# Leaky sum kept in PSUM with its low half on VectorE, second conversions behind the next row maxima, and a respread transition and last step

## The chip, the cores and the metric

The kernel runs on one core of one Trainium2 chip. The metric is the device time of one launch in microseconds (us), given as the median of several runs. The engines are TensorE (PE in the profile, its weight loads PEld), VectorE (DVE), ScalarE (ACT), GpSimd (POOL) and SyncE (SP, which issues the DMAs).

## The reference

Sliding-window attention over 2 batches, 8 heads, 768 positions and head size 64, followed by two feed-forward layers over the 1536 tokens (512 wide, 2048 hidden). All is float32 to the reader of the output; the four weight matrices arrive as 64-bit floats.

```python
scores = scale * np.matmul(q, k.transpose(0, 1, 3, 2)) + bias          # bias: -slope[h] * distance
scores = np.where(is_global | is_local, scores, -1000000000.0)         # 8 global keys, the last 96 positions
a = np.exp(scores - np.max(scores, axis=-1, keepdims=True))
attn = np.matmul(a / (np.sum(a, axis=-1, keepdims=True) + 1e-09), v)
x = attn.transpose(0, 2, 1, 3).reshape(B * S, H * D)
h = x @ moe_w_in                                                       # layer 1
x = (np.maximum(h, 0.0) + alpha * np.minimum(h, 0.0)) @ moe_w_out
h = x @ moe2_w_in                                                      # layer 2
g = (a0 + a1*h + a2*h*h + a3*h*h*h) / (1 + |b0|*|h| + |b1|*h*h + 1e-6)
out = g @ moe2_w_out
```

## The kernel before

**Products.** Each float32 operand is held as a high and a low half of a reduced format, and a product is three passes: high times high, low times high, high times low. The high half is a copy into that format on ScalarE, the low half a subtraction.

**Steps.** A step is one block of 128 hidden columns for one group of 512 tokens. There are 96: 48 of layer 1, then 48 of layer 2, grouped into runs over the same tokens. `first(n)` is the step's product with w_in: 12 matmuls into one PSUM bank `h` (bank 3 for the first 16 steps, later banks 0 to 2 in rotation). Then comes the nonlinear part: in layer 1 `leaky(n)`, in layer 2 the `rational_*` functions, called a, u, b, c, p, d, h, e here (a, u, c, h on ScalarE, b, p, d on VectorE, e on GpSimd). Both end in a high half `ghi` and a low half `glo`. `second(n)` is the product with w_out, 12 matmuls into banks 4 to 7, which add up over a run. At a run's end `drain` takes the four banks out; in a run's last step `second` finishes bank after bank and so wants the low half with its third matmul. Where a run's sum is part of an earlier one (`adds`), VectorE adds the saved part (L826), ScalarE copies the high half, and the low half (L835) is put off into the queue `later`.

**Slots.** The order of every engine's instructions is written out by hand (`tc.manual_schedule`), and each engine works its own list in order. While attention runs, slot s of 16 (`joint_slot`) issues: `opening` (scores of the next rows, reciprocals L472 and row maxima L447 of VectorE, exponentials L454 of ScalarE, values), `first(s)`, a tick, `turning` (transposes of the probabilities, their copies out, the split of new keys and queries L408 and L411), `leaky(s)`, `second(s-1)`, a tick. Afterwards a plain slot s issues `first(s)`, the nonlinear part of step s-1 and the end of that of s-2, a tick, `second(s-2)`, a tick. `final_slot` does the last step in two column halves.

**Ticks and conversions.** There are two ticks to a slot, number 2s and 2s+1. A tick moves the conversion of weights on: a 64-bit block of 128 x 512 is scaled by ScalarE (L324) in the tick at which it starts, joined into float32 by three VectorE instructions (L313, L314, L315) in the next, copied to its high half by ScalarE (L301) in the third and subtracted for its low half by VectorE (L304) in the fourth. `plan_weights` lists the ticks at which the blocks start; for layer 2 these are `times`. A tick also takes one entry from `later`.

The instructions of `leaky` are L741 and L742 on VectorE, L743 on ScalarE, L744 on GpSimd; those of `rational_d` L777 to L779, of `rational_h` L782, of `rational_e` L786.

Of the kernel before, what the change touches and what calls it, by code (L numbers as in the profile page):

```python
# [60 lines left out]
class Kernel:  # L61
# [35 lines left out]
    def arm(self, attention, sfx):  # L97
        tc = self.tc
        self.sfx = sfx
        self.slots = list(self.early)  # L100
        self.pipe, self.join, self.unspilled, self.later, self.splits = (deque() for _ in range(5))
        self.loads = self.started = self.used = 0
        moe = self.moe()
        with tc.tile_pool(name="spill_" + sfx, bufs=1, space=DRAM) as spill:
            self.spilled = [self.alloc_slot(spill, i, "d") for i in range(KEPT)]
            self.saved = {mg: spill.tile([P, NC, DM], F32, name=f"saved{mg[0]}{mg[1]}_{sfx}") for mg in SAVED}
            with tc.tile_pool(name="at_" + sfx, bufs=1) as pool:
                attention(pool, moe)
            with tc.tile_pool(name="late_" + sfx, bufs=1, reuse_waits="tile") as late:
                self.slots += [self.alloc_slot(late, i) for i in range(NEARLY, NF)]  # L110
                moe(None)
# [109 lines left out]
    def plan_weights(self):  # L221
        self.steps = [(0, 0, fc, fc % NEARLY) for fc in range(CH)]
        self.steps += [(0, 1, fc, fc % NEARLY) for fc in (*range(NEARLY, CH), *range(NEARLY))]
        self.steps += [(0, 2, fc, fc) for fc in range(NF)]
        self.steps += [(0, g, fc, fc) for g in (0, 1) for fc in range(CH, NF)]
        self.steps += [(1, g, j, j) for g in (2, 0) for j in range(CH)]
        self.steps += [(1, 1, j, j) for j in range(NF)]
        self.steps += [(1, g, j, j) for g in (2, 0) for j in range(CH, NF)]
        runs = [s[:2] for s in self.steps]
        self.begins = {n for n in range(len(runs)) if n == 0 or runs[n - 1] != runs[n]}  # L230
        self.ends = {n - 1 for n in self.begins if n} | {len(runs) - 1}
        self.saves = {n for n in self.ends if runs[n] in runs[n + 1 :]}
        self.adds = {n for n in self.ends - self.saves if runs[n] in SAVED}
        jobs = {}
        for fc in range(CH):
            jobs[2 * fc - 5 if fc > 2 else 2 * fc - 10] = 0, fc, "in", fc % NEARLY
            jobs[2 * fc - 2 if fc else -5] = 0, fc, "out", fc % NEARLY
        half, layer = NGR * CH, NGR * NF
        spare = [(fc, kind) for fc in range(CH, NF) for kind in ("in", "out")]
        for t, (fc, kind) in enumerate(spare):  # L240
            jobs[11 + 2 * t if fc < KEPT else 15 + 2 * t] = 0, fc, kind, None if fc < KEPT else fc
        todo = []
        for n, free in ((0, LATE), (CH, layer - CH)):
            for k in range(CH):
                for kind, lag in (("in", 0), ("out", 5)):
                    todo.append((n + k, 2 * (free + k) + lag, kind))
        times = [t for t in range(48, 96) if (t % 2 == 0 or t in (55, 71) or t > 82) and t not in (64, 66, 80, 82, 85, 88, 91, 94, 95)]
        times += range(101, 160, 5)
        for t in times:
            ready = [x for x in todo if x[1] <= t]  # L250
            if ready:
                j, _, kind = job = min(ready)
                todo.remove(job)
                jobs[t] = 1, j, kind, j
        assert not todo
        self.starts = set(jobs)
        self.plan = [jobs[t] for t in sorted(jobs)]
# [25 lines left out]

    def tick(self, on_act, start, spread=False):
        nc = self.nc
        if self.later:
            self.later.popleft()()
        while self.splits:
            self.splits.popleft()()
# [431 lines left out]
    def moe(self):  # L721
# [16 lines left out]
        def leaky(n):  # L738
            fc, h = steps[n][2], hbank.pop(n)
            t, hi, lo = self.act[n % 2], self.ghi[n % 2], self.glo[n % 2]  # L740
            nc.vector.tensor_scalar(t, h, 0.0, self.al[:, fc : fc + 1], ALU.min, ALU.mult)  # L741
            nc.vector.scalar_tensor_tensor(t, h, 0.0, t, ALU.max, ALU.add)  # L742
            nc.scalar.copy(hi, t)  # L743
            nc.gpsimd.tensor_tensor(lo, t, hi.bitcast(F32), ALU.subtract)  # L744

        def rational_parts(n):
            p = flat[NST - 2 + n % 2]
# [62 lines left out]
        def drain(n, d):  # L810
            m, g = steps[n][:2]
            y, o, r0 = banks[4 + d], self.part[d], g * GT + d * P
            out = self.out[r0 : r0 + P, :]
            if n in self.saves:
                if n < LATE - 1:
                    o = self.first_saved[d]
                (nc.vector.tensor_copy if d == 3 and m else nc.scalar.copy)(o, y)  # L817
                nc.sync.dma_start(out=self.saved[m, g][:, d, :], in_=o)
                return
            if n == N - 1 and d == 3:  # L820
                for half in (slice(0, DM // 2), slice(DM // 2, DM)):
                    nc.vector.tensor_add(o[:, half], y[:, half], o[:, half])
                    nc.sync.dma_start(out=out[:, half], in_=o[:, half])
                return
            if n in self.adds:
                nc.vector.tensor_add(o, y, o)  # L826
            elif m:
                (nc.vector.tensor_copy if d == 3 else nc.scalar.copy)(o, y)
            if m:
                nc.sync.dma_start(out=out, in_=o)  # L830
                return
            xh, xl = self.xhi[g][:, d, :], self.xlo[g][:, d, :]
            if n in self.adds:
                nc.scalar.copy(xh, o)
                self.later.append(lambda: nc.vector.tensor_sub(xl, o, xh.bitcast(F32)))  # L835
            else:
                nc.scalar.copy(xh, y)
                nc.vector.tensor_sub(xl, y, xh.bitcast(F32))
# [6 lines left out]
        def joint_slot(s, halves):  # L845
# [4 lines left out]
            if s == LATE - 1:  # L850
                self.spill()
            opening(u)
            first(s)
            self.tick(True, 2 * s in self.starts)
            lows = turning(u)
            leaky(s)
            for low in lows:
                low()
            if s:
                second(s - 1)  # L860
            self.tick(True, 2 * s + 1 in self.starts)

        def plain_slot(s):
            early, late = s - 1, s - 2
            fetch(s + 1)
            if CH <= s - LATE + CH - 2 < KEPT:
                self.reload(s - LATE + CH - 2)
            if s < N:
                first(s)
            if s >= N:  # L870
                final_slot(s)
                return
# [10 lines left out]
                rational_b(early)  # L883
            if late >= LATE and steps[late][0]:
                rational_e(late)
            if ready and not steps[early][0]:
                leaky(early)
            self.tick(True, 2 * s in self.starts)
            if ready and steps[early][0]:
                rational_c(early)  # L890
                rational_p(early)
# [83 lines left out]
```

## Time and profile before

| what | value |
|---|---|
| median of 3 runs | 663.15 us (661.48 to 663.91) |
| the profiled execution | 662.42 us |
| its span, first to last instruction | 660.6 us |
| TensorE busy | 622.9 us, 94% of the span |
| VectorE busy | 541.1 us, 82% |
| ScalarE busy | 374.8 us, 57% |
| GpSimd busy | 191.6 us, 29% |

The span is read on the slowest core, here the only one. Busy shares are means over the span; the stages have different limits, so the stretches of single slots tell more than the totals. A matmul's duration overlaps the next one's, so TensorE is read by its start times and by the waits in front of its instructions.

### The profile page before, as it was taken

How to read it: one execution, taken by the hardware profiler on the slowest of the kernel's cores; microseconds unless marked ns; L12 is line 12 of the kernel's file. 1: busy time of each engine (PE TensorE's matmuls, PEld its weight loads, DVE VectorE, ACT ScalarE, POOL GpSimd, SP SyncE). 2: the span in 40 equal slices, each digit the busy share in tenths (PEclk: the TensorE clock that was granted, in tenths of full speed). 3: DMA queues.
4: the chain of work that ended last, by engine and by line, in shares of the span. 5: the costliest groups of instructions: out<-in, count | busy, mean ns of one | idle time of the engine just before them, and what ended most of it. 6: DMA issues, size and time to landing. Idle time of an engine off the chain costs nothing. (4 is left out here: it accounts for less than half of the span.)

```text
span 660.6 us, 9551 instructions
## 1 busy us (share of the span) xinstructions
PE 622.9 (94%) x3250; PEld 506.3 (77%) x3250; DVE 541.1 (82%) x972; ACT 374.8 (57%) x782; POOL 191.6 (29%) x268
## 2 busy tenths in 40 slices
PE   6777998999999999999999998999999999999994
PEld 6566766778878888888888877878878888888783
DVE  4687899987656987977889999999989877786984
ACT  2785565667643432333333376777777666766662
POOL 4454434333341321222222212222222222222221
PEclk7998999999999999999999999999999999999998
DMA  8879498978777952330522511131110000300302
GB/s 162 192 189 274 145 256 261 269 207 268 255 263 253 353 183 90 103 96 32 165 90 65 158 34 33 36 125 32 33 64 1 1 1 1 127 1 0 129 0 70
DMA packets 84859, 82.82 MB, mean 125 GB/s; under 512 B 45312, under 2 KB 61952, under 8 KB 84800
## 3 DMA queue, kind: packets, MB, share of 16 engines
q1 hardware_dynamic: 84800, 82.11, 41.6%
q8 instruction: 27, 0.44, 0.3%
q14 instruction: 32, 0.26, 0.1%
HBM read 60.21 MB, written 19.92 MB: 121 GB/s over the span
## 5 line engine op out<-in xcount | busy, mean ns | idle before, releaser
L744 POOL TENSOR_TENSOR glo<-act,ghi 128x512 fp32r<-128x512 f32 x48 | 65.6, 1366 | 213.5 <-ACT ghi L743 193.8
L786 POOL TENSOR_TENSOR glo<-act,ghi 128x512 fp32r<-128x512 f32 (+1 forms) x49 | 65.3, 1332 | 201.9 <-ACT ghi L782 180.3
L743 ACT CAST ghi<-act 128x512 fp32r<-128x512 f32 x48 | 29.8, 621 | 104.6 <-DVE act L742 96.7
L735 PE MATMUL bank<-xhi,winhi_f 128*128 128x512 f32 x256 | 68.4, 389 | 0.0
L735 PE MATMUL bank<-xhi,winlo_f 128*128 128x512 f32 x256 | 68.4, 389 | 0.0
L735 PE MATMUL bank<-xlo,winhi_f 128*128 128x512 f32 x256 | 68.4, 389 | 0.0
L454 ACT ACTIVATE prob<-prob,stat 128x232 f32<-128x232 f32 (+1 forms) x96 | 44.7, 468 | 40.2 <-DVE stat L447 40.0
L735 PEld LDWEIGHTS bank<-xhi,winhi_f 128*128 128x128 f32 x256 | 48.1, 188 | 10.0
L735 PEld LDWEIGHTS bank<-xlo,winhi_f 128*128 128x128 f32 x256 | 48.1, 188 | 10.0
L735 PEld LDWEIGHTS bank<-xhi,winlo_f 128*128 128x128 f32 x256 | 48.1, 188 | 10.0
L314 DVE SCALAR_TENSOR_TENSOR dx<-de,dx 128x512 int32<-128x512 int32 x64 | 52.7, 824 | 2.2
L315 DVE SCALAR_TENSOR_TENSOR dx<-stage,dx 128x512 int32<-128x512 int32 x64 | 52.1, 815 | 2.2
L762 DVE SCALAR_TENSOR_TENSOR stage<-stage,abs_b 128x512 f32<-128x512 f32 (+1 forms) x49 | 36.2, 739 | 16.3 <-ACT stage L754 16.3
L753 ACT ACTIVATE stage<-bank 128x512 f32<-128x512 f32 (+1 forms) x49 | 28.8, 587 | 35.7 <-PE bank L735 35.7
L466 POOL TENSOR_SCALAR prob<-prob,rec 128x232 f32<-128x232 f32 (+1 forms) x96 | 42.2, 458 | 16.9 <-DVE rec L472 10.2
L782 ACT CAST ghi<-act 128x512 fp32r<-128x512 f32 (+1 forms) x49 | 30.2, 616 | 27.7 <-DVE act L779 27.7
L324 ACT ACTIVATE de<-stage 128x512 f32<-128x512 f32 x64 | 42.6, 671 | 2.6 <-DMA stage<-in_moe_w_out_dram 2.6
L801 PE MATMUL bank<-wouthi_f,glo 128*128 128x512 f32 x144 | 41.3, 392 | 0.8 <-POOL glo L786 0.7
L801 PE MATMUL bank<-wouthi_f,ghi 128*128 128x512 f32 x144 | 41.3, 392 | 0.6 <-ACT ghi L782 0.6
L313 DVE TENSOR_SCALAR dx<-de 128x512 int32<-128x512 int32 x64 | 38.6, 603 | 3.5 <-ACT de L324 3.5
L801 PE MATMUL bank<-woutlo_f,ghi 128*128 128x512 f32 x144 | 41.0, 389 | 0.0
L777 DVE SCALAR_TENSOR_TENSOR stage<-stage,cq,bank 128x512 f32<-128x512 f32 (+1 forms) x49 | 36.0, 734 | 4.1 <-ACT bank L767 4.1
(208 smaller groups left out, 1466.7 us busy)
## 6 DMA issues: line engine op xcount, KB each, us to landing
stage<-in_moe_w_in_dram SPq DMA_DIRECT2D x32, 512.0 KB, 3.9
stage<-in_moe_w_out_dram SPq DMA_DIRECT2D x32, 512.0 KB, 4.1
part<-saved_f SPq DMA_DIRECT2D x16, 256.0 KB, 4.0
va<-in_v_dram SPq DMA_DIRECT2D x13, 256.0 KB, 5.1
saved_f<-part SPq DMA_DIRECT2D x12, 256.0 KB, 3.5
out_dram<-part SPq DMA_DIRECT2D x11, 256.0 KB, 2.0
rawk<-in_k_dram SPq DMA_DIRECT2D x10, 256.0 KB, 4.6
rawq<-in_q_dram SPq DMA_DIRECT2D x10, 256.0 KB, 4.7
```

The lines of the kernel that those rows point to most:

```text
L313: lambda: nc.vector.tensor_scalar(y, e, 3, None, ALU.logical_shift_left),
L314: lambda: nc.vector.scalar_tensor_tensor(y, e, -(2**31), y, ALU.bitwise_and, ALU.bitwise_or),
L315: lambda: nc.vector.scalar_tensor_tensor(y, low, 29, y, ALU.logical_shift_right, ALU.bitwise_or),
L324: nc.scalar.mul(self.de[n % 2], self.staged(n)[:, :, :, 1].bitcast(F32), 2.0**-112)
L454: nc.scalar.activation(p[:, j - e, :w], p[:, j - e, :w], AF.Exp, bias=st[:, j : j + 1], scale=-1.0, accum_out=st[:, 4 + j : 5 + j],)
L466: nc.gpsimd.tensor_scalar(p[:, j, :w], p[:, j, :w], r[:, e + j : e + j + 1], 1.0, ALU.mult, ALU.mult)
L735: nc.tensor.matmul(bk, w["in", a][:, c, :], x[:, c, :], start=e == 0, stop=e == len(seq) - 1)
L744: nc.gpsimd.tensor_tensor(lo, t, hi.bitcast(F32), ALU.subtract)
L762: nc.vector.scalar_tensor_tensor(w, w, self.ab[:, 0:1], ab, ALU.add, ALU.mult)
L777: nc.vector.scalar_tensor_tensor(w, w, self.cq[:, 0:1], r, ALU.add, ALU.mult)
L786: nc.gpsimd.tensor_tensor(lo, u, hi.bitcast(F32), ALU.subtract)
L801: nc.tensor.matmul(y[d], lhs, rhs, start=begin and e == 0, stop=last and e == 2)
```

## The change

- `leaky` writes its sum back into the PSUM bank of `h`. ScalarE copies the high half from there, and the low half is a VectorE subtraction that reads that bank; GpSimd has no part in it any more. The function hands that subtraction back, and the caller places it: in a joint slot behind the low halves of keys and queries, in a plain slot behind the first tick.
- The odd tick of a joint slot stands behind the next slot's `opening` and not at the slot's end.
- `later` gives one entry at every other tick.
- The last conversions of layer 2 start at ticks 107, 112, ... and not 101, 106, ...
- `first` of the last step is issued one slot earlier.
- The last half block of the output is sent by ScalarE's DMA queue.

```diff
-        times += range(101, 160, 5)
+        times += range(107, 160, 5)
...
-        if self.later:
+        self.ticks += 1
+        if self.later and self.ticks % 2:
             self.later.popleft()()
...
             nc.vector.tensor_scalar(t, h, 0.0, self.al[:, fc : fc + 1], ALU.min, ALU.mult)
-            nc.vector.scalar_tensor_tensor(t, h, 0.0, t, ALU.max, ALU.add)
-            nc.scalar.copy(hi, t)
-            nc.gpsimd.tensor_tensor(lo, t, hi.bitcast(F32), ALU.subtract)
+            nc.vector.scalar_tensor_tensor(h, h, 0.0, t, ALU.max, ALU.add)
+            nc.scalar.copy(hi, h)
+            return lambda: nc.vector.tensor_sub(lo, h, hi.bitcast(F32))
...
-                    nc.sync.dma_start(out=out[:, half], in_=o[:, half])
+                    (nc.scalar if half.start else nc.sync).dma_start(out=out[:, half], in_=o[:, half])
...
             opening(u)
+            if s:
+                self.tick(True, 2 * s - 1 in self.starts)
             first(s)
             self.tick(True, 2 * s in self.starts)
             lows = turning(u)
-            leaky(s)
-            for low in lows:
-                low()
+            low = leaky(s)
+            for more in lows:
+                more()
+            low()
             if s:
                 second(s - 1)
-            self.tick(True, 2 * s + 1 in self.starts)
+            if s == LATE - 1:
+                self.tick(True, 2 * s + 1 in self.starts)
...
-            if s < N:
+            if s < N - 1:
                 first(s)
+            if s == N - 2:
+                first(s + 1)
...
-            if ready and not steps[early][0]:
-                leaky(early)
+            low = leaky(early) if ready and not steps[early][0] else None
             self.tick(True, 2 * s in self.starts)
+            if low:
+                low()
```

In the changed file the same lines stand one number higher up to `leaky`'s, and its subtraction is L745.

VectorE at the seam of two joint slots, before: the leaky sum, the split of a query, then a conversion, then the next slot's reciprocals and row maxima.

```order
L742 SCALAR_TENSOR_TENSOR act_99<-bank_85,act_99 128x512
L411 SCALAR_TENSOR_TENSOR qlo_253<-bank_84,qhi_251 128x512
L304 TENSOR_TENSOR woutlo__122<-dx_96,wouthi__121 128x512
L313 TENSOR_SCALAR dx_98<-de_94 128x512
L314 SCALAR_TENSOR_TENSOR dx_98<-de_94,dx_98 128x512
L315 SCALAR_TENSOR_TENSOR dx_98<-stage_90,dx_98 128x512
L472 RECIPROCAL rec_263<-rec_263 128x4
L447 ISA prob_256,stat_261<-bank_82,bm_284 128x128
```

The same seam in the change, up to the last row maximum.

```order
L743 SCALAR_TENSOR_TENSOR bank_85<-bank_85,act_99 128x512
L412 SCALAR_TENSOR_TENSOR qlo_253<-bank_84,qhi_251 128x512
L745 TENSOR_TENSOR glo_103<-bank_85,ghi_101 128x512
L473 RECIPROCAL rec_263<-rec_263 128x4
L448 ISA prob_256,stat_261<-bank_82,bm_284 128x128
```

The conversion (now L305, L314 to L316) has moved behind the row maxima and the attention's low half, and `glo` is a VectorE instruction that reads bank_85, which is bank 3.

TensorE in the last three slots, before: the last step's first product (bank_84) stands behind step 92's second product, whose first matmul and last matmul are shown.

```order
L735 MATMUL bank_83<-xlo_108,winhi_f 128x512 x4
L801 MATMUL bank_86<-wouthi_f,ghi_101 128x512
...
L801 MATMUL bank_89<-wouthi_f,glo_103 128x512
L735 MATMUL bank_84<-xhi_105,winhi_f 128x512 x4
```

In the change:

```order
L736 MATMUL bank_83<-xlo_108,winhi_f 128x512 x4
L736 MATMUL bank_84<-xhi_105,winhi_f 128x512 x4
L736 MATMUL bank_84<-xhi_105,winlo_f 128x512 x4
L736 MATMUL bank_84<-xlo_108,winhi_f 128x512 x4
L802 MATMUL bank_86<-wouthi_f,ghi_101 128x512
```

The product into bank_84 has moved ahead of the twelve matmuls into banks 86 to 89.

VectorE at the layer change, before: the four sums of the drain, the first low half of `later`, then the three instructions of `rational_d`.

```order
L826 TENSOR_TENSOR part_78<-bank_89,part_78 128x512
L835 TENSOR_TENSOR xlo_109<-part_75,xhi_106 128x512
L777 SCALAR_TENSOR_TENSOR stage_92<-stage_92,cq,bank_85 128x512
L778 SCALAR_TENSOR_TENSOR stage_92<-stage_92,bank_85 128x512
L779 SCALAR_TENSOR_TENSOR act_99<-act_99,na,stage_92 128x512
L762 SCALAR_TENSOR_TENSOR stage_93<-stage_93,abs_b 128x512
L835 TENSOR_TENSOR xlo_109<-part_76,xhi_106 128x512
```

In the change:

```order
L827 TENSOR_TENSOR part_78<-bank_89,part_78 128x512
L778 SCALAR_TENSOR_TENSOR stage_92<-stage_92,cq,bank_85 128x512
L779 SCALAR_TENSOR_TENSOR stage_92<-stage_92,bank_85 128x512
L780 SCALAR_TENSOR_TENSOR act_99<-act_99,na,stage_92 128x512
L763 SCALAR_TENSOR_TENSOR stage_93<-stage_93,abs_b 128x512
L836 TENSOR_TENSOR xlo_109<-part_75,xhi_106 128x512
```

The first low half now follows `rational_d`, and the second has moved a slot on.

## Rows read from the trace of the kernel before

**Rows 1.** Windows by slot without attention: stretch, length, busy time per engine, PEclk, DMA.
```profile
300.57:306.01 5.44, 5.44 (x26) 4.50 (x24) 4.06 (x7) 1.89 (x4) 1.29 (x1) 1.00 0.00 0
...
387.61:394.86 7.25, 5.75 (x26) 4.43 (x24) 7.14 (x12) 6.77 (x13) 1.63 (x1) 1.00 0.00 0
...
400.36:407.99 7.63, 5.76 (x26) 4.43 (x25) 7.46 (x12) 5.83 (x10) 1.63 (x1) 1.00 0.24 69
429.75:436.20 6.45, 5.78 (x26) 4.43 (x24) 6.19 (x10) 3.97 (x8) 1.62 (x1) 1.00 0.26 92
441.64:447.45 5.81, 5.75 (x26) 4.43 (x24) 5.67 (x10) 3.93 (x8) 1.30 (x1) 1.00 0.29 90
480.13:485.96 5.83, 5.75 (x25) 4.37 (x24) 4.69 (x6) 4.59 (x9) 1.69 (x1) 1.00 0.46 155
485.96:492.54 6.58, 5.78 (x26) 4.43 (x25) 6.41 (x11) 5.32 (x10) 1.64 (x1) 1.00 0.00 0
601.34:606.77 5.43, 5.43 (x25) 4.50 (x24) 4.28 (x7) 3.52 (x7) 1.29 (x2) 1.00 0.00 0
```

**Rows 2.** Windows by slot, attention running, same columns.
```profile
99.57:109.67 10.10, 8.70 (x55) 6.38 (x53) 9.45 (x22) 6.06 (x18) 3.21 (x7) 1.00 0.93 266
...
158.35:167.26 8.91, 8.91 (x67) 7.30 (x65) 6.12 (x17) 5.71 (x16) 3.63 (x7) 1.00 0.98 284
```

**Rows 3.** Timeline of the slot at 99.57: start, us, engine, line, operands.
```profile
99.12 1.56 POOL L744 TENSOR_TENSOR glo<-act,ghi 128x512 fp32r<-128x512 f32 x1 [4.94 <-ACT ghi L743]
99.44 1.52 DVE L313 TENSOR_SCALAR dx<-de 128x512 int32<-128x512 int32 x1
...
102.33 0.17 DVE L472 RECIPROCAL rec<-rec 128x4 f32<-128x4 f32 x1
...
102.59 1.41 POOL L466 TENSOR_SCALAR prob<-prob,rec 128x128 f32<-128x128 f32 x4 [1.58 <-PE bank L735]
...
102.71 0.39 DVE L447 CUSTOM_DVE_ANT_0 prob<-bank,bm 128x232 f32<-128x232 f32 x1
...
105.17 0.42 DVE L313 TENSOR_SCALAR dx<-de 128x512 int32<-128x512 int32 x1
```

**Rows 4.** Groups by shape: busy us, mean ns, idle before.
```profile
L408 DVE TENSOR_TENSOR klo<-bank,khi 128x512 fp32r<-128x512 f32 x11 | 7.5, 685 | 3.1 <-ACT khi L407 3.0
```

**Rows 5.** Timeline of ScalarE in the slot of the last first product.
```profile
640.37 0.58 ACT L767 ACTIVATE bank<-bank 128x512 f32<-128x512 f32 x1
```

**Rows 6.** Timeline of VectorE in the slot at 79.43.
```profile
82.68 0.18 DVE L472 RECIPROCAL rec<-rec 128x4 f32<-128x4 f32 x1 [1.15 <-POOL rec L471]
```

**Rows 7.** Timeline of the slot at 158.35, with one conversion.
```profile
159.06 0.18 DVE L472 RECIPROCAL rec<-rec 128x4 f32<-128x4 f32 x1 [1.79 <-POOL rec L471]
...
161.31 0.68 DVE L304 TENSOR_TENSOR spare<-dx,spare 128x512 fp32r<-128x512 f32 x1
...
161.70 0.19 ACT L454 ACTIVATION_READ_ACCUMULATOR prob<-prob,stat 128x1 f32 x1
...
164.47 0.69 DVE L742 SCALAR_TENSOR_TENSOR act<-bank,act 128x512 f32<-128x512 f32 x1
```

**Rows 8.** Timeline of the layer change.
```profile
391.99 1.20 PE L801 MATMUL bank<-wouthi__113,ghi 128*128 128x512 f32 x4 [1.50 <-ACT ghi L782]
...
397.88 1.52 DVE L313 TENSOR_SCALAR dx<-de 128x512 int32<-128x512 int32 x1
...
400.78 0.68 DVE L772 TENSOR_TENSOR act<-act,bank 128x512 f32<-128x512 f32 x1
...
405.11 1.19 PE L801 MATMUL bank<-wouthi__121,ghi 128*128 128x512 f32 x4 [1.87 <-ACT ghi L782]
```

**Rows 9.** Timeline of the end.
```profile
642.83 0.38 ACT L753 ACTIVATE stage<-bank 128x256 f32<-128x256 f32 x1 [1.88 <-PE bank L735]
...
652.17 0.39 PE L801 MATMUL bank<-wouthi_f,glo 128*128 128x512 f32 x1
...
653.07 1.44 SPq L823 DMA_DIRECT2D out_dram<-part  x2
```

More of the change, by code (lines that the diff above doesn't have):

```diff
@@ L101, in arm @@
         self.pipe, self.join, self.unspilled, self.later, self.splits = (deque() for _ in range(5))
-        self.loads = self.started = self.used = 0
+        self.loads = self.started = self.used = self.ticks = 0
         moe = self.moe()
```

## Prediction

> **What bounds the kernel now.** I first read the windows by slot, because the stages have different limits. A plain slot (no attention) has 24 matmuls of 512 columns; in the typical ones at 300.57 and 601.34 TensorE is busy for all of 5.44 us, 0.2267 each, and nothing on another engine can shorten that [rows 1]. Six slots are longer: 7.25 and 7.63 us around the change of layer, 6.45 and 5.81, then 5.83 and 6.58 where the first two runs of layer 2 end. Their excess over 5.44 is 1.81 + 2.19 + 1.01 + 0.37 + 0.39 + 1.14 = 6.9 us. While attention runs the picture differs [rows 2]: the slot at 99.57 takes 10.10 us with TensorE busy for 8.70, and the slot at 158.35 takes 8.91 with TensorE busy throughout. The difference is the conversions: two per slot in the former, one in the latter.
>
> Second, the order of events in that 10.10 us slot [rows 3]. VectorE is busy 9.45 of 10.10 us [rows 2]; it is the limit there. One item is odd: the first conversion's L313 takes 1.52 us, the second's 0.42, for the same shape. The long one starts at 99.44, while GpSimd's subtraction L744 runs from 99.12 to 100.68, and it ends 0.28 after that. So GpSimd's low half costs VectorE 1.10 us per slot.
>
> Third, the timelines of the layer change and of the end, where each wait of TensorE has a releaser by name.
>
> **The low half on VectorE.** Removed: 48 GpSimd subtractions, 1.56 us each in rows 3, which lie beside other work but hold L313 for 1.10 us. Added: 48 VectorE subtractions with one input in PSUM and one in SBUF, output in SBUF. The nearest row is L408, the same kind: 0.685 us [rows 4]; behind others such an instruction starts about 0.6 after the one before it. The lower bound is 0.42 (the free L313, one input), the upper 1.52 (the held one) [rows 3]; I take 0.6. It also waits for ScalarE's copy of the high half, which starts only when L742 is done. L411 or L408 stands between and hides 0.6 of the copy's 0.6, so with the two hand-overs I allow 0.2. VectorE writing PSUM is in no row; between L408's 0.685 and L313's 1.52 I take no change, since ScalarE's pass from PSUM into PSUM, L767, takes 0.58 [rows 5] and shows no surcharge for that target.
>
> [...]
>
> Sum for a slot with two conversions: 10.10 - 1.10 + 0.6 + 0.2 = 9.8 us. In seven such slots (68 to 140 us) that is 7 x 0.3 = 2.1 us less.
>
> **The conversion behind the row maxima.** L472 and the four L447 now stand ahead of L313 to L315. GpSimd's normalisation L466, and with it TensorE's transposes, come some 2 us earlier in the slot; TensorE's wait in front of them goes. But the leaky sum now stays in bank 3 until the low half is read, and every joint slot's first product writes bank 3. In the old order first(s) started at 99.57, 2.8 us before L472 at 102.33 [rows 3]; in the new one it cannot start before the low half is done, just where L472 starts. So TensorE's wait moves from the transposes to first(s), and VectorE's 9.8 us stays the period. One slot pays more: at 82.68 L472 waits 1.15 us for GpSimd's copies of the global keys [rows 6]; the conversion that ran ahead of it is now behind, so VectorE stands idle about 1.3 us longer there. Joint stage: -2.1 + 1.3 = -0.8 us.
>
> For slots with one conversion I followed the same ring [rows 7]. ScalarE's exponentials end 2.83 us after L472 (161.89 - 159.06); the weight's high half, one ScalarE pass of about 0.6, now follows them and L304 waits for it, at +3.45; from L304's start to L742's end it is 3.85 (165.16 - 161.31); then copy 0.6 and the low half 0.6 to the next L472: 3.45 + 3.85 + 0.1 + 0.6 + 0.6 = 8.6 us. That is below 8.91, so these slots stay with TensorE. GpSimd no longer delays L471, which frees nothing that TensorE waits for here. In plain slots of layer 1 the added 0.6 is covered: TensorE takes 5.44 and VectorE 4.06 in the row at 300.57 [rows 1], and three banks rotate. Without that cover it would be 33 x 0.6 = 20 us.
>
> **Layer change.** `later` now gives one low half per slot, from the slot after the drains. Before, one L835 stands directly ahead of the three instructions that end in ScalarE's L782 (the order rows above show it), for which TensorE waits 1.50 us at 391.99 [rows 8]; taking it away brings 0.6. The conversion of tick 101, L313 at 397.88 to the next instruction at 400.78, is 2.9 us of VectorE ahead of the wait of 1.87 at 405.11; it moves three slots on, and the four L835 cost 0.6 in each of four slots where VectorE has about 1.1 to spare (5.44 less 4.28 at 601.34 [rows 1]). That slot loses its whole excess of 2.19. Together -2.8 us.
>
> **Runs' ends in layer 2.** All remaining conversions start six ticks later. Before, VectorE is exactly late at 405.11 and two conversions follow (ticks 106, 111) while a slot gives back 1.1 at most; so it is late again at 429.75, where a run's last second product asks for the low half at once. Now it is not late at 405, gains 0.5 to 1.1 in each of three slots without a conversion, and has some 2 us in hand there: -1.0. The conversion of tick 116, first after the drains, becomes that of 117, one slot further from them: -0.4 at 441.64. After the second run's drains tick 131 becomes 132, whose L313 to L315 fall into an odd tick, where GpSimd is not subtracting: -0.4 and -1.0 [rows 1]. In return the conversion started at tick 127 now falls just ahead of that run's last second product (near 477), where none was: +0.9. Sum -1.9, from 0 (all of it only moves) to -2.9.
>
> **The last step.** Its first product is issued before second(92) and not after it, so it ends 2.7 us earlier, at 639.9. ScalarE waited 1.88 us for it at 642.83 and was free from 640.95 (640.37 + 0.58) [rows 5, 9]. So the rational chain starts 1.9 us earlier; the VectorE work of step 94 (777 to 779, 2.2 us) then stands in its way, and I take 1.1 for the high half. TensorE's 24 matmuls from 645.35 need 5.44 and would end at 650.8; the last one now starts at 652.17, ending 1.6 later. I take 1.3 of that. The last half block leaves by ScalarE's queue: the two issues are 1.44 us together on SP [rows 9]; the second one's data are ready 0.2 before its turn. ScalarE's issue is in no row; between 0 and 0.7 (half of that pair) I take -0.2. Sum -1.5.
>
> **Sum.** -0.8 - 2.8 - 1.9 - 1.5 = -7.0 us from the profiled execution's 662.42 us (its span is 660.6, with 1.8 around it), so 655.4. That execution lies 0.7 below the median 663.15 and inside the three runs' spread; I name 655.5.
>
> **Rivals.** (a) The layer 2 waits only move along with the conversions, and the joint stage gives nothing: 662.4 - 2.8 - 1.5 = 658.1. For it: each conversion keeps its length, and VectorE is full in those slots. Against: the positions relative to the drains do change. (b) The lock stays: another GpSimd instruction holds a conversion for as long as L744 did. The four L466 of a slot are 1.41 us together [rows 3]. Then a slot is 10.9 instead of 9.8: 7 x 1.1 = 7.7 on top, 663.1, no change. Against: L466 follows L472, while VectorE runs L447 from PSUM; the L447 at 102.71 lies wholly beside L466 (102.59 to 104.00) and takes 0.39. [...] (c) Slower: the ring through bank 3. If the copy of the high half comes late, because ScalarE works off both weight copies and both probability copies ahead of it, first(s) waits directly. Its margin there is thin, an estimate: L742 ends at +8.5 (9.8 less copy, low half and hand-over), and ScalarE, which waits for the first conversion's L315 until +4.7 (1.9 to L520, then 0.3 + 0.6 + 1.9), has five passes of 0.6 ahead of the copy, until +7.7: 0.8 us. If the ring is 11.0 in seven slots and 10.0 in six, it costs 7 x 0.9 + 6 x 1.1 = 12.9 against the old periods; 662.4 + 12.9 - 6.2 = 669.1. It decides from about 1 us of lateness per slot. (d) The new order saves the lock and hides the added part: 7 x 1.1 = 7.7 instead of 0.8 in the joint stage, 648.5.
>
> **Chances.** Forecast 0.62 (its own range 652.5 to 658), (a) 0.17, (b) 0.09, (c) 0.07, (d) 0.05. A measurement here tells about 0.5% from no change, 3.3 us. Faster is the forecast, (a) and (d), less a tail: 0.81; same is (b) and that tail: 0.12; slower is (c): 0.07. The range leaves out (d), (c) and the far part of (b): 651 to 660.5.
>
> **What would show it.** Right: L313 in 67 to 131 us at 0.42 each; TensorE waiting for the low half before a joint slot's first product and no longer before the transposes; joint slots near 9.8; no wait over 0.3 at the second slot after the layer change; TensorE's last matmul 1.3 us closer to its count. Wrong: joint slots of 10.1 or more, a TensorE wait of more than 1.5 us anywhere between the layer change and 540 us, or a longer GpSimd lock.

## The result, and the profile after

The changed kernel takes 653.25 us (median of 4 runs, 651.66 to 654.45) and the kernel before, in 4 runs, 663.53 (661.48 to 664.06). The ratio is 0.9849, with a 95% interval of 0.9819 to 0.9879. The forecast was 655.5 us with a range of 651.0 to 660.5. The profiled execution after takes 651.66 us with a span of 649.9, so 10.7 us left the span where 7.0 were forecast.

Where they left it is read from the starts of the first products. The table gives the stretches between them in both profiles, "start" being the time up to step 0's first product and "end" the time from step 94's to the last instruction.

| stretch, by steps | before | after | difference | forecast |
|---|---|---|---|---|
| start | 61.23 | 59.85 | -1.38 | 0 |
| 0 to 8 (attention, mostly two conversions) | 79.18 | 75.60 | -3.58 | -0.8 |
| 8 to 16 (attention, one conversion) | 64.96 | 64.88 | -0.08 | 0 |
| 16 to 50 | 182.24 | 182.24 | 0 | 0 |
| 50 to 56 (layer change) | 36.71 | 33.90 | -2.81 | -2.8 |
| 56 to 69 (ends of layer 2's first runs) | 73.66 | 72.17 | -1.49 | -1.9 |
| 69 to 94 | 136.49 | 136.51 | 0 | 0 |
| end | 26.15 | 24.76 | -1.39 | -1.5 |

Three of four terms hold to within about 0.4 us; the joint stage (steps 0 to 16) gives 2.9 us more than its term, and the start 1.4 that no edit touches. The windows by slot after, with the columns of [rows 1] and [rows 2]:

```profile
77.93:86.87 8.94, 8.92 (x66) 7.29 (x64) 8.07 (x18) 5.71 (x15) 1.39 (x5) 1.00 1.11 307
86.87:96.11 9.24, 8.15 (x55) 6.42 (x53) 8.37 (x21) 5.80 (x17) 1.47 (x5) 1.00 0.84 255
96.11:105.87 9.76, 8.19 (x52) 6.41 (x53) 9.05 (x24) 6.19 (x17) 1.75 (x5) 1.00 1.00 283
...
382.56:389.26 6.70, 5.73 (x25) 4.43 (x24) 6.56 (x11) 6.55 (x12) 1.59 (x1) 1.00 0.00 1
...
394.70:400.14 5.44, 5.44 (x25) 4.50 (x24) 5.33 (x9) 3.80 (x7) 1.63 (x1) 1.00 0.00 0
...
421.90:427.34 5.44, 5.44 (x25) 4.50 (x24) 5.33 (x8) 3.98 (x7) 1.29 (x1) 1.00 0.31 117
...
465.54:471.94 6.40, 5.74 (x25) 4.43 (x24) 6.17 (x10) 3.94 (x7) 1.62 (x1) 1.00 0.25 89
471.94:477.38 5.44, 5.44 (x25) 4.50 (x24) 4.81 (x7) 5.41 (x11) 1.29 (x1) 1.00 0.49 163
477.38:483.19 5.81, 5.74 (x26) 4.43 (x24) 5.67 (x10) 3.94 (x8) 1.30 (x1) 1.00 0.29 92
```

The first row is the slot that was to get longer (step 2, 10.75 us before): it is now 8.94. The third answers to the 10.10 of [rows 2]. In layer 2 the slots that were 7.25, 7.63 and 6.45 in [rows 1] are 6.70, 5.44 and 5.44; 480.13 and 485.96, 5.83 and 6.58 there, are now the last two rows; and the slot at 465.54 has the new wait that was forecast for it.

The timeline of the slot at 96.11 after:

```profile
98.81 0.42 DVE L314 TENSOR_SCALAR dx<-de 128x512 int32<-128x512 int32 x1
...
101.20 0.42 DVE L314 TENSOR_SCALAR dx<-de 128x512 int32<-128x512 int32 x1
...
104.38 0.68 DVE L412 SCALAR_TENSOR_TENSOR qlo<-bank,qhi 128x512 fp32r<-128x512 f32 x1
104.50 0.59 ACT L744 CAST ghi<-bank 128x512 fp32r<-128x512 f32 x1 [1.55 <-DVE bank L743]
105.12 0.66 PE L508 MATMUL bank<-pt,va 128*64 128x128 f32 x8 [1.48 <-DVE qlo L412]
105.12 0.69 DVE L745 TENSOR_TENSOR glo<-bank,ghi 128x512 fp32r<-128x512 f32 x1
105.73 0.17 DVE L473 RECIPROCAL rec<-rec 128x4 f32<-128x4 f32 x1
...
105.87 1.20 PE L736 MATMUL bank<-xhi,winhi__115 128*128 128x512 f32 x4
```

Both conversions now begin with 0.42 us, where one took 1.52 in [rows 3]. ScalarE's copy (L744) lies beside L412, and the low half L745 follows L412 without a gap. TensorE's list of waits while two conversions run (total us, times, longest), first before (61 to 140 us), where L483 are the transposes of the probabilities, then after (59 to 136 us):

```profile
PE bank L483 <- DVE stat L447: 2.4, 3, 1.1
PE bank L483 <- POOL prob L466: 2.1, 3, 1.0
```

```profile
PE bank L508 <- DVE klo L409: 2.9, 3, 1.1
PE bank L508 <- DVE qlo L412: 2.6, 3, 1.5
PE bank L736 <- ACT xhi L520: 0.2, 1, 0.2
```

The waits in front of the transposes are gone. A wait now stands at the values product L508, not at the first product L736. L508 starts with the leaky low half and runs as long as it; L736 follows 0.06 us after L745's end.

GpSimd's timeline before, where the copies of the global keys (L415) stand behind L744 and [rows 6] show L472 waiting 1.15 us after them; then GpSimd's and VectorE's after, with the first and the last of the ten copies and the reciprocal that answers to the one of [rows 6]:

```profile
78.11 1.61 POOL L744 TENSOR_TENSOR glo<-act,ghi 128x512 fp32r<-128x512 f32 x1 [4.74 <-ACT ghi L743]
79.67 0.40 POOL L415 CAST khi<-khi 128x32 fp32r<-128x32 f32 x1
```

```profile
69.67 0.21 POOL L416 CAST khi<-khi 128x32 fp32r<-128x32 f32 x1
...
71.75 0.21 POOL L416 CAST klo<-klo 128x32 fp32r<-128x32 f32 x1
...
76.94 0.17 DVE L473 RECIPROCAL rec<-rec 128x4 f32<-128x4 f32 x1
```

The copies (L416 now) run from 69.67 on, a whole slot earlier, and the reciprocal waits for nothing.

### The profile page after: what moved, and what is told of

Same layout as the page of the kernel before. It is cut to its first block, busy times and chain, and to the rows that moved or that the text cites. A ratio compares the mean times of both kernels' runs of the same rounds, so it can differ in the third digit from the quotient of the medians.

```text
span 649.9 us, 9514 instructions
## 1 busy us (share of the span) xinstructions
PE 617.3 (95%) x3250; PEld 507.1 (78%) x3250; DVE 538.7 (83%) x1020; ACT 375.5 (58%) x782; POOL 127.1 (20%) x220
## 5 line engine op out<-in xcount | busy, mean ns | idle before, releaser
L787 POOL TENSOR_TENSOR glo<-act,ghi 128x512 fp32r<-128x512 f32 (+1 forms) x49 | 65.7, 1341 | 385.4 <-ACT ghi L783 372.6
L744 ACT CAST ghi<-bank 128x512 fp32r<-128x512 f32 x48 | 28.3, 589 | 110.4 <-DVE bank L743 92.8
L736 PE MATMUL bank<-xhi,winhi_f 128*128 128x512 f32 x256 | 68.4, 389 | 0.0
L736 PE MATMUL bank<-xhi,winlo_f 128*128 128x512 f32 x256 | 68.4, 389 | 0.0
L736 PE MATMUL bank<-xlo,winhi_f 128*128 128x512 f32 x256 | 68.4, 389 | 0.0
L736 PEld LDWEIGHTS bank<-xhi,winlo_f 128*128 128x128 f32 x256 | 48.1, 188 | 10.0
L736 PEld LDWEIGHTS bank<-xhi,winhi_f 128*128 128x128 f32 x256 | 48.1, 188 | 10.0
L736 PEld LDWEIGHTS bank<-xlo,winhi_f 128*128 128x128 f32 x256 | 48.1, 188 | 10.0
L315 DVE SCALAR_TENSOR_TENSOR dx<-de,dx 128x512 int32<-128x512 int32 x64 | 48.6, 760 | 2.2
L745 DVE TENSOR_TENSOR glo<-bank,ghi 128x512 fp32r<-128x512 f32 x48 | 33.1, 689 | 16.8 <-ACT ghi L744 9.4
L316 DVE SCALAR_TENSOR_TENSOR dx<-stage,dx 128x512 int32<-128x512 int32 x64 | 44.3, 693 | 2.2
L742 DVE TENSOR_SCALAR act<-bank,al 128x512 f32<-128x512 f32 x48 | 35.8, 745 | 9.7 <-PE bank L736 9.7
```

The costliest lines, as they stand in the source:

```text
L315: lambda: nc.vector.scalar_tensor_tensor(y, e, -(2**31), y, ALU.bitwise_and, ALU.bitwise_or),
L316: lambda: nc.vector.scalar_tensor_tensor(y, low, 29, y, ALU.logical_shift_right, ALU.bitwise_or),
L736: nc.tensor.matmul(bk, w["in", a][:, c, :], x[:, c, :], start=e == 0, stop=e == len(seq) - 1)
L745: return lambda: nc.vector.tensor_sub(lo, h, hi.bitcast(F32))
L787: nc.gpsimd.tensor_tensor(lo, u, hi.bitcast(F32), ALU.subtract)
```

## The experiments

Each text quoted below is what was expected before its run. Theory A: the joint stage gains because GpSimd's subtraction is gone, by its hold on VectorE's conversion and by its place in GpSimd's own queue; the moved tick adds nothing, and layer change and end gain by their own edits. Rival B: the moved tick makes the joint gain, or the edits need each other. One table holds the stretches of all runs; the texts below refer to it.

| kernel | start | 0 to 8 | 8 to 16 | 50 to 56 | 56 to 69 | end |
|---|---|---|---|---|---|---|
| before | 61.23 | 79.18 | 64.96 | 36.71 | 73.66 | 26.15 |
| after | 59.85 | 75.60 | 64.88 | 33.90 | 72.17 | 24.76 |
| leaky alone | 61.31 | 75.56 | 64.44 | 36.71 | 73.61 | 26.15 |
| tick alone | 62.32 | 84.93 | 70.36 | 36.77 | 73.63 | 26.70 |
| low half from SBUF | 60.61 | 75.72 | 64.45 | 36.71 | 73.61 | 26.34 |
| keys ahead | 62.20 | 78.02 | 64.98 | 38.29 | 72.67 | 26.85 |
| key and query lows first | 61.29 | 83.87 | 66.92 | 33.90 | 72.20 | 24.79 |
| transition alone | 60.06 | 79.17 | 64.97 | 34.05 | 72.17 | 26.42 |
| first product early | 60.64 | 79.16 | 65.00 | 36.72 | 73.58 | 25.80 |
| change without the tick | 59.77 | 75.53 | 64.43 | 33.90 | 72.16 | 24.84 |
| negative part on ScalarE | 61.99 | 72.65 | 64.43 | 33.90 | 72.15 | 24.64 |
| the same, tick 126 | 60.46 | 72.67 | 64.43 | 33.90 | 71.39 | 24.48 |

**Leaky alone.** The kernel before with this edit and its places in the slots:

```diff
-            nc.vector.scalar_tensor_tensor(t, h, 0.0, t, ALU.max, ALU.add)
-            nc.scalar.copy(hi, t)
-            nc.gpsimd.tensor_tensor(lo, t, hi.bitcast(F32), ALU.subtract)
+            nc.vector.scalar_tensor_tensor(h, h, 0.0, t, ALU.max, ALU.add)
+            nc.scalar.copy(hi, h)
+            return lambda: nc.vector.tensor_sub(lo, h, hi.bitcast(F32))
```

> The kernel before with one part of the change alone: the leaky sum in PSUM and its low half on VectorE. From the first product of step 0 to that of step 8 the kernel before takes 79.2 us, the change 75.6. Theory A (the gain of the joint stage comes from taking the GpSimd subtraction away: no lock on L313, and the key copies of the slot at 79.43 no longer queue behind it): 76 to 76.5 here, that slot near 9 instead of 10.76, the slots after it near 9.8. Rival B (the gain comes from the conversion behind the row maxima): 78.5 to 79.5. Total by A 3 us under before, by B no difference.

658.72 us, ratio 0.9943 (0.9921 to 0.9964). Slots 0 to 8 take 75.56, a little below A's 76: the whole gain of the joint stage is in this edit, and slots 8 to 16 gain 0.5 besides. B falls here. The seven instructions L313 that took 1.51 to 1.52 us in the joint slots before are back to 0.42 to 0.50.

**Tick alone.** The kernel before with the odd tick behind the next opening:

```diff
             opening(u)
+            if s:
+                self.tick(True, 2 * s - 1 in self.starts)
             first(s)
...
-            self.tick(True, 2 * s + 1 in self.starts)
+            if s == LATE - 1:
+                self.tick(True, 2 * s + 1 in self.starts)
```

> The kernel before with the odd tick of a joint slot moved behind the next slot's opening, the leaky sum as before. Theory A: the lock goes too (the GpSimd subtraction then lies beside the row maxima, which it does not hold), but L472 waits for GpSimd's L471, which still queues behind the subtraction, about 1.7 us of idle VectorE per slot: step 0 to step 8 in 78 to 81 us. Rival B: 76.

675.93 us, ratio 1.0199 (1.0179 to 1.0220): slower by 13 us, 5.75 in slots 0 to 8 and 5.4 in slots 8 to 16. The direction is A's, the size beyond its 78 to 81. The timeline at the seam of two slots:

```profile
112.38 0.68 DVE L411 SCALAR_TENSOR_TENSOR qlo<-bank,qhi 128x512 fp32r<-128x512 f32 x1
112.55 0.62 ACT L743 CAST ghi<-act 128x512 fp32r<-128x512 f32 x1 [1.61 <-DVE act L742]
113.25 1.28 POOL L744 TENSOR_TENSOR glo<-act,ghi 128x512 fp32r<-128x512 f32 x1 [7.60 <-ACT ghi L743]
114.62 0.19 POOL L471 TENSOR_SCALAR rec<-stat 128x4 f32<-128x4 f32 x1
114.85 0.18 DVE L472 RECIPROCAL rec<-rec 128x4 f32<-128x4 f32 x1 [1.79 <-POOL rec L471]
```

With the conversion moved away, nothing of VectorE lies beside this L744 (113.25 to 114.53), and in the slot at 102.82 VectorE is busy for 8.45 us, 1.00 less than in the 10.10 us slot of [rows 2], near the 1.10 of the held L313, though L744 is still there. So it is the overlap that holds it. No row maximum lies beside it either (the first starts at 114.95), so whether it would hold one is not shown. But L471, which feeds the reciprocal, stands behind L744 in GpSimd's queue, and VectorE idles 1.79 us for it. Before, the conversion filled that time. The move is a loss unless L744 leaves GpSimd. A part of the 13 us may be TensorE's clock: 0.97 and 0.98 of its full speed are granted over the two stretches, 1.00 before.

**Low half from SBUF.** As "leaky alone", but the sum goes to `t` in SBUF as before, and VectorE subtracts from there:

```diff
-            nc.gpsimd.tensor_tensor(lo, t, hi.bitcast(F32), ALU.subtract)
+            return lambda: nc.vector.tensor_sub(lo, t, hi.bitcast(F32))
```

> The kernel before, with the low half of the leaky sum as a VectorE subtraction, placed as in the change, but with the sum itself left in SBUF as before: the subtraction then has both inputs in SBUF. Theory A (the gain of the joint slots is the absence of GpSimd's subtraction; where the sum lies matters little): slots 0 to 8 at 75.6 us, as with the leaky edit alone, slots with two conversions 9.7 to 9.9. Rival B (both inputs in SBUF make VectorE and GpSimd wait for each other, as L313 waited for L744): one of L744 or the normalisations L466 takes over 1 us and the slots with two conversions are 10.1 or more, slots 0 to 8 at 78 or more.

658.51 us, ratio 0.9930 (0.9905 to 0.9956), slots 0 to 8 at 75.72. Which memory holds the sum makes no difference that shows, though the slot of step 5 (10.23) lies outside A's range. B's wait is not tested here: in none of the 48 steps does a GpSimd instruction run beside this subtraction. The subtraction takes 690 ns on average from SBUF and 689 from PSUM; ScalarE's copy 621 and 589.

**Keys ahead.** The kernel before, with the copies of the global keys issued one slot earlier, ahead of that slot's L744:

```diff
             scores(u)
-            keys_of_all(u)
+            if u == JOIN // 2:
+                keys_of_all(u)
...
                 lows.append(split_in(nm, i, 2, cs))
+            keys_of_all(u + 1)
             return lows
```

> The kernel before, in which only the copies of the global keys are issued one slot earlier, ahead of the GpSimd subtraction of that slot. Theory A: the slot at 79.43 falls from 10.76 to between 9.0 and 9.7 and the other joint slots stay (step 0 to step 8 in 77.4 to 78.2). If those copies are not what delays that slot, it stays at 10.7.

663.62 us in a single run. The slot of step 2, before and in this run:

```profile
79.43:90.19 10.76, 9.62 (x67) 7.17 (x65) 8.81 (x22) 6.05 (x17) 5.78 (x17) 1.00 0.87 243
```

```profile
80.41:90.01 9.60, 9.60 (x66) 7.17 (x64) 8.80 (x22) 6.03 (x17) 3.35 (x7) 1.00 0.92 264
```

It loses 1.15 us (10.75 to 9.60, before rounding), exactly the wait of [rows 6], and the other joint slots stay. So 1.15 of the 1.81 us that this slot gains in the change are the copies' new place. The stretches 50 to 56 and 56 to 69 differ from before by +1.6 and -1.0 in this one execution. The +1.6 is all in the slot of step 52, and there the clock fell (1.00 in [rows 1] at 400.36):

```profile
406.00:408.00 2.00, 2.00 (x6) 1.54 (x5) 1.93 (x4) 1.98 (x4) 0.63 (x1) 0.50 0.00 0
```

TensorE had been busy for 1.03 and 1.07 us of the two stretches of 2 us in front of this one. The -1.0 is in the slot of step 57, which takes 5.44 here.

**Key and query lows first.** The change, with L409 and L412 ahead of the leaky sum:

```diff
-            low = leaky(s)
             for more in lows:
                 more()
+            low = leaky(s)
             low()
```

> The change, with the low halves of keys and queries (bank 2) ahead of the leaky sum on VectorE instead of behind it. In the change TensorE waits before the values product for them in the slots of steps 3 to 7, period 9.76 to 10.04. If VectorE is the limit there, the wait moves to the first product (bank 3) and the period stays within 0.15. If the late release of bank 2 is the limit, the period falls by about 0.6 in five slots, 3 us together.

663.52 us in a single run: 10.3 us above the change's median, and neither theory expected it. TensorE's waits from 61 to 140 us, and the timeline at one seam:

```profile
PE bank L736 <- DVE glo L745: 8.5, 7, 2.0
```

```profile
111.17 0.70 DVE L743 SCALAR_TENSOR_TENSOR bank<-bank,act 128x512 f32<-128x512 f32 x1
...
111.90 0.59 ACT L744 CAST ghi<-bank 128x512 fp32r<-128x512 f32 x1 [2.16 <-DVE bank L743]
...
112.52 0.69 DVE L745 TENSOR_TENSOR glo<-bank,ghi 128x512 fp32r<-128x512 f32 x1 [0.65 <-ACT ghi L744]
...
113.26 0.95 PE L736 MATMUL bank<-xhi,winhi__115 128*128 128x512 f32 x3 [0.68 <-DVE glo L745]
```

Without L412 beside it the copy is uncovered: VectorE waits 0.65 us, and the first product waits for the bank, 8.5 us in seven slots. That is the ring of rival (c), which the change's own order just avoids, but not by (c)'s cause: ScalarE is not late, it has been idle for 2.16 us when it starts the copy. A part may be TensorE's clock: over slots 0 to 8, in which it waits this often, 0.96 of its full speed is granted here and 1.00 in the change.

**Transition alone.** The kernel before with the starts at 107, 112, ... and `later` at every other tick:

```diff
-        times += range(101, 160, 5)
+        times += range(107, 160, 5)
...
-        if self.later:
+        self.ticks += 1
+        if self.later and self.ticks % 2:
```

> The kernel before, with two edits alone: the last conversions start at ticks 107, 112, ... and the queue of low halves gives one entry at every other tick. Theory A (the layer change gains by itself, as forecast): from the first product of step 50 to that of 56 33.9 us in place of 36.7 (-2.8), from 56 to 69 72.2 in place of 73.7 (-1.5), and the joint slots and the end as before: about 659.2, 4.3 less than before. Rival B (the gain there rests on the leaky sum or on the start of the conversions in the joint slots): less than 1.5 us in all, above 662. The wait of about 1 us near the slot of step 65 appears in A, since the conversion of tick 127 falls there.

658.56 us, ratio 0.9933 (0.9909 to 0.9957): 34.05 us from step 50 to 56 and 72.17 from 56 to 69. A holds; the gain needs nothing of the joint stage. The run moves both edits together, so which of them gives which part was not tested.

**First product early.** The kernel before with this edit alone:

```diff
-            if s < N:
+            if s < N - 1:
                 first(s)
+            if s == N - 2:
+                first(s + 1)
```

> The kernel before, with one edit alone: the first product of the last step is issued one slot earlier; both half blocks of the output still leave by SyncE's queue. Theory A (the earlier first product carries the whole gain of the end but for the queue): from the first product of step 94 to the last instruction 24.9 us in place of 26.15 (-1.25), and the queue is worth 0.1 to 0.2 of the 1.39 measured for both; all else as before, total about 662.2. Rival B (the gain of the end is the queue's): 26.0 or more.

661.16 us, ratio 0.9969 (0.9957 to 0.9981). The end takes 25.80, between the two expectations. Its parts explain it: from step 94's first product to the start of the last matmul 16.43 us, against 17.70 before and 16.44 after, but 9.37 from there to the last instruction, against 8.45 and 8.32. The first part is the edit's and holds; the second is the tail of the output's DMAs, which differs from profile to profile (see "The end" below).

**Change without the tick.** The odd tick stands at the slot's end again:

```diff
             opening(u)
-            if s:
-                self.tick(True, 2 * s - 1 in self.starts)
             first(s)
...
-            if s == LATE - 1:
-                self.tick(True, 2 * s + 1 in self.starts)
+            self.tick(True, 2 * s + 1 in self.starts)
```

> The changed kernel without one of its edits: the odd tick of a joint slot stands at the slot's end again. Theory A (the move of the tick gives nothing; the joint stage gains by the low half on VectorE alone): slots 0 to 8 at 75.6 us and slots 8 to 16 at 64.4 (0.4 less than in the change, as with the leaky edit alone), layer change and end as in the change: within 1 us of the changed kernel, about 652.8. Rival B (the move is what lets the other edits pay): over 655.

651.70 us, ratio 0.9829 (0.9807 to 0.9851), not to be told from the change in total, whose interval it overlaps. Slots 8 to 16 take 64.43 in place of 64.88: the moved tick costs 0.4 us there (8.03 in place of 7.60 in step 13's slot) and gives nothing in slots 0 to 8.

**Negative part on ScalarE.** From the kernel just shown, VectorE's pass L742 is replaced by one of ScalarE, which makes max(-h, 0); `om` holds 1 - alpha:

```diff
-            nc.vector.tensor_scalar(t, h, 0.0, self.al[:, fc : fc + 1], ALU.min, ALU.mult)
-            nc.vector.scalar_tensor_tensor(h, h, 0.0, t, ALU.max, ALU.add)
...
+            nc.vector.scalar_tensor_tensor(h, t, self.om[:, fc : fc + 1], h, ALU.mult, ALU.add)
...
+        def negative(n):
+            nc.scalar.activation(self.act[n % 2], hbank[n], AF.Relu, scale=-1.0)
...
+            negative(s)
             lows = turning(u)
```

> The change without the tick's move, and the first VectorE pass of the leaky sum taken away: ScalarE makes max(-h, 0) ahead of its copies of the probabilities (0.6 us), and one VectorE pass adds it, times 1 - alpha, to h in the bank. Theory A (in slots with two conversions VectorE's own length sets the period): the seven slots lose up to 0.7 each, down to TensorE's 9.0, from 9.76 to about 9.1; slots 0 to 8 at 72 (71 to 73), slots 8 to 16 as before at 64.4, total about 648.3. Rival B (the chain of ScalarE's exponentials, probability copies and key copies takes VectorE's place, as it gets 0.6 more): slots 0 to 8 at 75 or more, total 651.5 or more.

650.31 us, ratio 0.9816 (0.9803 to 0.9830). The slots of steps 4 and 5 in its windows:

```profile
97.18:106.25 9.07, 8.69 (x54) 6.37 (x53) 8.38 (x22) 6.54 (x18) 1.74 (x5) 1.00 1.02 293
106.25:115.75 9.50, 9.40 (x66) 7.17 (x64) 8.40 (x22) 6.87 (x18) 2.09 (x5) 1.00 0.98 305
```

VectorE's length was the period: with 0.7 us less of it (8.38 for 9.05) slots 0 to 8 lose 2.9 us, where 3.5 were expected. The slot of step 3 loses 1.0 and that of step 4 the 0.7; those of steps 5 to 7 lose only 0.3 to 0.5 and stay at 9.43 to 9.50, 0.5 to 0.6 above a slot with one conversion, with VectorE no longer full. No wait of TensorE's matmuls over 0.3 us is listed there, but one of its weight loads, ahead of the transposes (106 to 135 us):

```profile
PEld bank L486 <- POOL prob L469: 2.1, 6, 0.5
```

These are the probabilities that GpSimd normalises, 2.1 us in the three slots, whose excess over 8.90 is 1.7. It points at GpSimd's place in the order as the next limit; no run tests it.

**The same, with the start at tick 127 moved to 126.**

```diff
-        times += range(107, 160, 5)
+        times += [107, 112, 117, 122, 126, *range(132, 160, 5)]
```

> The kernel with ScalarE's pass in the leaky sum, and one start of the last conversions moved from tick 127 to 126. Theory A (the wait of about 1 us near the slot of step 65 is the conversion of tick 127, whose VectorE part stands ahead of the run's last second product): from the first product of step 61 to that of step 69 43.9 us in place of 44.86, the slot of step 65 at 5.44 to 5.5 in place of 6.40, all else as in the kernel beside it, 0.9 us less. Rival B (it only moves the wait to a neighbouring slot): 44.6 or more for these eight slots.

648.71 us, ratio 0.9796 (0.9782 to 0.9809), whose interval lies below that of the change (both against the kernel before): this version beats both kernels. The slot of step 65 and the one behind it:

```profile
462.77:468.43 5.66, 5.66 (x25) 4.43 (x24) 5.24 (x8) 3.97 (x8) 1.30 (x1) 1.00 0.08 30
468.43:473.87 5.44, 5.44 (x25) 4.50 (x24) 4.83 (x8) 5.41 (x11) 1.29 (x1) 1.00 0.47 163
```

5.66 in place of 6.36 in the kernel beside it, and 0.73 less in steps 61 to 69 (44.11 for 44.84), a little under the 0.9 expected. The wait was that conversion's, and it did not move on. The rest of the 1.6 us between the two medians is not in these slots; the two profiles differ by 1.5 in the start.

## Why the prediction was right, and where a term was off

**The lock and its price, right.** L313 (now L314) is 0.41 to 0.45 us between 67 and 131 us, the next instruction starts 0.61 behind the subtraction's start (0.6 forecast), and the copy is covered by L409 or L412. The slots of steps 4 to 7 are 9.76, 10.04, 9.76 and 9.77, where 9.8 was forecast. VectorE is busy for 9.05 of 9.76, and its list of waits from 96.11 to 135.44 has one entry, 0.5 us a slot:

```profile
DVE xlo L521 <- ACT xhi L520: 1.9, 4, 0.5
```

"Negative part on ScalarE" shows that its length is the period, "low half from SBUF" that it makes no difference which memory holds the sum (690 ns for the subtraction from SBUF, 689 from PSUM). Without the slot of step 2 the slots of steps 1 to 7 lose 1.79 us together, where 6 x 0.3 = 1.8 was forecast. The sum is right, the even share is not: two of them lose 0.14, the others 0.33 to 0.50. (The prediction counts 33 plain slots of layer 1; there are 32. No term rests on it.)

The lock also held instructions with two inputs in SBUF (L304, L314, L315), and outside the joint stage: beside L744, 30 of VectorE's conversion instructions took 1.05 to 1.80 us in the slots of steps 16 to 50 before. In the change none of them takes over 0.69, and yet this stretch takes 182.24 in all twelve kernels: there VectorE has time to spare (4.06 of 5.44 us in [rows 1]). The gain came where VectorE is the limit.

**The mis-sized term: the slot of step 2.** The step "the conversion that ran ahead of it is now behind, so VectorE stands idle about 1.3 us longer there" gave -0.3 + 1.3 = +1.0; measured is -1.81. The difference of 2.8 is all but 0.1 of the miss of the joint stage. I left the key copies where [rows 6] had them. They stood there only because L744 stood ahead of them in GpSimd's queue, waiting for the leaky sum; with L744 gone they run at 69.67, a slot earlier. "Keys ahead" makes 1.15 of it by that place alone; the 0.66 that remain, down to 8.94, where TensorE is busy for 8.92, come with the rest of the leaky edit.

**The new order behind the row maxima, half right.** The wait in front of the transposes is gone, and the first product starts as soon as the low half is out, as forecast. But the listed wait is the values product's, one product earlier, for the halves L409 and L412. "Key and query lows first" shows that the ring through bank 3 is real and how near it is: this order is 10.3 us behind the change's median. Rival (c) priced the ring at 12.9 against the old periods; against them slots 0 to 16 are 6.7 longer in this run. What I did not see is that the tick's move is worth nothing by itself: "leaky alone" has the joint gain without it, and with L744 still on GpSimd the kernel is 13 us slower.

**Slots with one conversion, right with two cancelling parts.** -0.08 is -0.5 from the low half ("leaky alone") and +0.4 from the tick ("change without the tick").

**Layer change, right.** -2.81 for -2.8. The first wait falls from 1.50 [rows 8] to 0.97, by 0.53 where 0.6 was forecast; the second is gone:

```profile
386.41 1.20 PE L802 MATMUL bank<-wouthi__113,ghi 128*128 128x512 f32 x4 [0.97 <-ACT ghi L783]
```

**Runs' ends, right but for 0.4.** The slots at 429.75 and 441.64 lose 1.0 and 0.4, that of step 66 0.4 and that of step 67 0.8 (1.0 forecast); step 65's pays 0.92 (0.9 forecast), and step 60's 0.1 more that was not. "Tick 126" shows that most of the price was avoidable. For steps 66 and 67 the forecast moved the conversion to where GpSimd is not subtracting. Before, L786 held one of its passes; after, the conversion still meets the end of L787 (474.44 to 475.73), and its first pass takes 0.79 in place of 0.42, which fits the part that is missing:

```profile
483.16 1.69 POOL L786 TENSOR_TENSOR glo<-act,ghi 128x512 fp32r<-128x512 f32 x1 [5.51 <-issue]
```

```profile
483.74 1.67 DVE L315 SCALAR_TENSOR_TENSOR dx<-stage,dx 128x512 int32<-128x512 int32 x1
```

```profile
475.22 0.79 DVE L314 TENSOR_SCALAR dx<-de 128x512 int32<-128x512 int32 x1
```

**The end, right.** The last matmul comes 1.26 us closer to step 94's first product (1.3). In the timeline after, ScalarE takes up the last step at 631.53 with no wait of its own, where it waited 1.88 in [rows 9], and issues the second half:

```profile
631.53 0.38 ACT L754 ACTIVATE stage<-bank 128x256 f32<-128x256 f32 x1
...
641.58 0.40 PE L802 MATMUL bank<-wouthi_f,glo 128*128 128x512 f32 x1
...
642.47 1.32 SPq L824 DMA_DIRECT2D out_dram<-part  x1
642.80 0.37 ACTq L824 DMA_DIRECT2D out_dram<-part  x1
```

The queue's 0.2 is 0.13 in this pair of executions, but the profile before, with that of "leaky alone", is the shortest of its kind here. From the last matmul's start to the last instruction the seven kernels with both issues on SyncE need 8.45 to 9.37 us (mean 8.82), the five with one on ScalarE 8.03 to 8.41 (mean 8.26): about 0.6 less on average.

**The parts add up, within wide intervals.** By their ratios the leaky edit gives 3.8 us of 663 (give or take 1.4), the transition 4.4 (1.6) and the early first product 2.1 (0.8), together 10.3; the whole change gives 10.0 (2.0). That it comes out so close is in part luck: the moved tick's 0.4 and the queue's 0.6 are in the whole alone. The stretches are the firmer sum: without the start they give 9.3 us less in the profile after, where 7.0 was forecast.

**The start is not the change's.** See the last section.

## What to carry to other kernels

When an instruction leaves an in-order queue, look at what stood behind it there and was ready: that moves up too (here the key copies, from 79.67 to 69.67 us), and waits read from the trace of before can vanish with it. Price a removed instruction by what it holds (here 1.10 us of another engine, and a copy waiting behind it), and test each edit alone: the kernel with the moved tick alone is 13 us slower, while in the change the move costs 0.4. Where two engines hand a bank to a third, name what covers the hand-over; here one 0.68 us instruction beside a 0.59 us copy decided some 10 us.

## What the runs showed of the hardware

No edit reaches the stretch before step 0, but for one small instruction in the last two kernels, yet it comes in two kinds. TensorE's granted clock over the first 20 us, from the windows of before and after (PEclk is the third column from the end):

```profile
0.00:20.00 20.00, 14.03 (x75) 12.53 (x75) 8.37 (x46) 6.30 (x19) 9.59 (x40) 0.74 0.87 156
```

```profile
0.00:20.00 20.00, 14.59 (x90) 12.44 (x90) 8.99 (x47) 7.04 (x21) 9.64 (x40) 1.00 0.87 156
```

0.74 is a mean over full speed and some 10 us at half of it (before, 0.50 is granted from 10 to 17.5 us). The six profiles with 0.74 reach step 0's first product at 61.23 to 62.32 us, the six with 0.83 to 1.00 at 59.77 to 60.64, with and without each edit. So some 1.4 us of the difference of two single profiles can be this, as here, and a median of few runs can hold part of it. That the clock is the cause is not shown: from 20 to 40 us the order is the other way about, with 0.91 to 1.00 in the first six and 0.83 to 0.91 in the others. What sets it off is open too.

SyncE's issue of the first half block (L823, L824 after) takes 0.40 us in the profile before and 1.09 to 1.32 in the other eleven. Where both issues are SyncE's, the second starts behind it: in the profile before at 653.57, the first taking 0.40 from 653.07. In the profile after ScalarE's starts at 642.80, while SyncE's runs from 642.47 to 643.79.
